# k^T v as the weight and q as the moving operand in the attention bursts of a fused attention and GLU kernel

## The chip, the cores and the metric

One Trainium2 chip, of which the kernel uses one core. The metric is device microseconds of one execution; before the change two runs took 1019.85 and 1017.05 us, median 1018.45. The profile is of one more execution, of 1019.05 us. Engines are named as in the profile: PE is TensorE, DVE VectorE, ACT ScalarE, POOL GpSimd; SP only issues DMAs.

## The reference

Linear attention without a softmax, an RMS norm over each head's 64 features, and a feed-forward layer whose gate is a sigmoid. All is fp32; the feed-forward weights come as 64-bit floats.

```python
def _attn_ref(q, k, v, g_norm):          # q, k, v: 8 batches, 8 heads, 576 tokens, 64 features
    kv = np.einsum('bhsd,bhse->bhde', k, v)
    out = np.einsum('bhsd,bhde->bhse', q, kv)
    rms = np.sqrt(np.mean(out * out, axis=-1, keepdims=True) + 1e-06)
    return (out / rms * g_norm).astype(np.float32)
...
def _moe_ref(x, w_gate, w_val, w_out):   # x: 4608 tokens x 512; 512 x 1536 twice; 1536 x 512
    gate = 1.0 / (1.0 + np.exp(-(x @ w_gate)))
    val = x @ w_val
    return (gate * val @ w_out).astype(np.float32)
```

x is the attention's output with the heads side by side: 4608 rows (8 batches of 576 tokens), 512 columns.

## The kernel before

The feed-forward runs in nine chunks of 512 tokens, c = 0 to 8. Chunk 0 is computed with plain matmuls while the 64-bit weights are turned to fp32. Chunks 1 to 8 use a fast form of matrix multiplication: each layer is split in blocks, and 26 products of sums of blocks take the place of 32. `first_layer_fast` (products at L932) runs 3 x 26 products, of two matmuls each with 256 moving columns; `second_layer_fast` (products at L1029) runs 26 products of three blocks. Sums of blocks of x, of the weights and of h are formed by DVE and GpSimd (L722, L741, L830, L1003), and the products are combined out of PSUM by DVE (L902) and ACT (L898, L891 for the sigmoid). Five PSUM banks go round among the products; three more are one tile, `at`, of the attention.

The attention of batches 0 and 1 is computed at the start, by `attention`. That of batches 2 to 7 is spread over the first and second layers of the chunks: `feed(b)` makes a list of steps, and chunk c carries those of batch c + 1 (so chunks 1 to 6 carry batches 2 to 7). Where a step goes is written out by hand: a pair (p, i) in `first` says that step i is issued after product p of the first layer, counted 0 to 77; the steps in `then` go after products of the second layer, and the lists X1, X2, X3 and `forms` place the sums of x and of weights in the same way. Every engine does its instructions in the order in which they were issued, so a step also holds its place in its engine's queue. A step after product p is issued behind that product's own combining work.

For each batch there are:

- `kv_mm` (L366, L372) and `kv_copies` (L377, ACT): k^T v of all eight heads into `at`, and from there to `kvq`, with k's features on partitions, 32 at a time;
- `turn` (L383): DVE transposes q in 32 x 32 blocks into `qTs`;
- `two_pairs(n0)`, twice, for two pairs of heads each: `u_mm` (L407) computes u = q (k^T v) with tokens on partitions, 72 matmuls with 32 rows of contraction, 64 columns of q as the weight and 64 columns of k^T v moving; `u_square` (L413, ACT), `u_sum` (L416, DVE, twice), `u_root` (L419, ACT), `u_norm` (a reciprocal at L423 and twice L425, DVE), and twice `x_turn`: DVE transposes of 32 x 32 blocks into `xTs` (L432), and DMAs on SP's queue (L442) that carry them to `xT_ring`, where the feed-forward reads x with features on partitions.

Since `at` is one tile, the second `u_mm` of a batch waits until the first pair's u has been read. The steps of the second `two_pairs` up to `u_norm` stand in the first layer, its two `x_turn` steps in the second layer. `load_q`, the stores of the output (L496, L503), and in chunk 1 the writes of the formed weights (L758, L1008) use SP's queue too; the streamed weights use GpSimd's (L770, L990).

Of the kernel before, what the change touches and what calls it, by code (L numbers as in the profile page):

```python
# [10 lines left out]
FP32 = mybir.dt.float32  # L11
# [3 lines left out]
AF = mybir.ActivationFunctionType  # L15
ALU = mybir.AluOpType
AX = mybir.AxisListType
# [3 lines left out]
def kernel(  # L21
# [11 lines left out]
    nc = tc.nc  # L33

    B, H, S, HD = q.shape
    T, DM = out.shape
    DF = moe_w_gate.shape[1]
    P = 128
    NHP = H // 2
    NJ = 6  # L40
    NP = S // NJ
    JH = NJ // 2


    PH = P // 2
# [5 lines left out]
    QB = 32  # L51
    NQ = NP // QB
    QC = QB * NJ
    NC = HD // QB
    XC = QB * JH
# [6 lines left out]
    G = 512  # L62
# [8 lines left out]
    const = ctx.enter_context(tc.tile_pool(name="const", bufs=1))  # L71
    sb = ctx.enter_context(tc.tile_pool(name="sb", bufs=2))
# [173 lines left out]

    qTs = const.tile([P, 2, 2 * NJ * HD], FP32, name="qTs")
    sqs = const.tile([P, 2 * NU * P], FP32, name="sqs")
    xTs = const.tile([P, NC, 2, S // 2], FP32, name="xTs")
    for e in range(2):  # L250
        nc.scalar.dma_start(out=g_col[HD * e:HD * e + HD], in_=g_norm.rearrange("(d o) -> d o", o=1))
    make_identity(nc, ident)
    nc.vector.memset(eps, 1e-6)

    nc.scalar.activation(out=sb.tile([P, 1], FP32, name="unused", bufs=1), in_=eps, func=AF.Sqrt)
# [2 lines left out]
    NX = 3  # L258
# [95 lines left out]
    def feed(b):  # L354
# [33 lines left out]
        def two_pairs(n0):  # L388


            d = {}
            ms = sb.tile([P, NQ, NJ], FP32, tag="ms2", name="ms2", bufs=1)
            sq = sqs[:, 0:2 * S].rearrange("p (r c) -> p r c", r=NQ)
            units = [slice(NJ // 2 * i, NJ // 2 * (i + 1)) for i in range(2)]

            def by_head(t):
                return t.rearrange("p r (n d) -> p r n d", d=HD)

            def u_mm():
                d["u"] = u = at_ps()[:, 0:NQ, 0:2 * QC]  # L400
                for which in range(2):
                    for g in range(JH):
                        for i in range(NC):
                            for r in range(NQ):
                                for e in range(2):
                                    c, o = NJ * HD * e + QC * i + PH * g, HD * (JH * which + g)
                                    nc.tensor.matmul(u[HD * e:HD * e + HD, r, o:o + HD],  # L407
                                                     qTs[QB * r:QB * r + QB, (n0 + which) % 2, c:c + PH],
                                                     kvq[QB * r:QB * r + QB, (n0 + which) % NHP, NC * e + i],
                                                     start=(i == 0), stop=(i == NC - 1))  # L410

            def u_square():
                nc.scalar.activation(out=sq, in_=d["u"], func=AF.Square)  # L413

            def u_sum(i):
                nc.vector.tensor_reduce(out=ms[:, :, units[i]], in_=by_head(sq)[:, :, units[i]], axis=AX.X, op=ALU.add)  # L416

            def u_root():
                nc.scalar.activation(out=ms, in_=ms, func=AF.Sqrt, bias=eps, scale=1.0 / HD)  # L419

            def u_norm(i):
                if i == 0:
                    nc.vector.reciprocal(ms, ms)  # L423
                m_ = ms[:, :, units[i]]
                nc.vector.tensor_tensor(out=by_head(sq)[:, :, units[i]], in0=by_head(d["u"])[:, :, units[i]],  # L425
                                        in1=m_.unsqueeze(3).to_broadcast([P, NQ, NJ // 2, HD]), op=ALU.mult)

            def x_turn(i):


                for which in range(2):
                    nc.vector.transpose(xTs[:, i, which],  # L432
                                        sq.rearrange("p r (w g i c) -> p w i r g c", w=2, g=JH, i=NC)[:, which, i])
                m = n0 % NHP
                for j in range(2):
                    for e in range(2):
                        p0, p1 = HD * e + QB * j, HD * e + QB * i
                        s0 = 0
                        while s0 < S // 2:
                            o = (S * b + S // 2 * j + s0) % (NX * G)  # L440
                            n_ = min(NX * G - o, S // 2 - s0)
                            nc.sync.dma_start(out=xT_ring[p1:p1 + QB, m:m + 2, o:o + n_],  # L442
                                                          in_=xTs[p0:p0 + QB, i, :, s0:s0 + n_])
                            s0 += n_

            return ([u_mm, u_square, lambda: u_sum(0), lambda: u_sum(1), u_root, lambda: u_norm(0), lambda: u_norm(1)] +
                    [lambda i=i: x_turn(i) for i in range(NC)])

        def turns_of(n):
            return [lambda n=n, e=e: turn(n, e) for e in range(2)]  # L450
# [3 lines left out]
        t0, t1, t2, t3 = (turns_of(n0 + i) for i in range(4))  # L454
        u0, u1 = two_pairs(n0), two_pairs(n0 + 2)
        steps_ = t0 + t1 + t2 + t3 + u0 + u1[:7]
        first = [(p, steps_[i]) for p, i in (((0, 0), (5, 1), (9, 2), (21, 3), (25, 8), (26, 9), (28, 4), (28, 5), (30, 10), (30, 11), (32, 6), (42, 12), (48, 13), (49, 7), (50, 14), (52, 15), (53, 16), (53, 17), (56, 18), (57, 19), (57, 20), (60, 21), (60, 22), (62, 23)) if b == 2 else
                                             ((4, 0), (8, 1), (24, 2), (24, 3), (28, 8), (29, 4), (29, 5), (30, 9), (32, 10), (33, 11), (35, 6), (37, 12), (41, 13), (47, 7), (47, 14), (51, 15), (51, 16), (53, 17), (56, 18), (56, 19), (56, 20), (60, 21), (60, 22), (65, 23)) if b == 3 else
                                             ((3, 0), (7, 1), (24, 2), (24, 3), (28, 8), (28, 4), (30, 5), (30, 9), (30, 10), (32, 11), (37, 12), (39, 6), (47, 13), (47, 7), (47, 14), (53, 15), (53, 16), (54, 17), (56, 18), (56, 19), (56, 20), (60, 21), (61, 22), (63, 23)))]
        return kv, first, u1[7:]  # L460

    def flush():
# [24 lines left out]
    def store(c, t, ot, cols=slice(0, DM), queues=(nc.sync,)):  # L487

        r0 = i = 0
        while r0 < P:  # L490
            b, s = divmod(G * c + P * t + r0, S)
            rows = out[S * b:S * b + S, cols]
            if b < 2:
                j, p = divmod(s, NP)
                n = min(P - r0, NP - p)
                queues[i % len(queues)].dma_start(out=rows.rearrange("(p j) d -> j p d", j=NJ)[j, p:p + n],  # L496
                                                  in_=ot[r0:r0 + n, cols])
            else:

                half, c0 = divmod(s, S // 2)  # L500
                r, c0 = divmod(c0, XC)
                n = QB
                queues[i % len(queues)].dma_start(  # L503
                    out=rows.rearrange("(r p g i) d -> i r g p d", p=QB, g=JH, i=2)[half, r, c0 // QB],
                    in_=ot[r0:r0 + n, cols])
            r0 += n
            i += 1

# [17 lines left out]
    def at_ps():  # L526
        return psum.tile([P, NQ, 512], FP32, tag="at", name="at")
# [567 lines left out]
        store(0, t, ot)  # L1095

    flush()
    X1 = (12, 16, 16, 17, 18, 18, 19, 19, 19, 20, 20, 21, 21, 24, 25, 25, 25, 25)
    X2 = (14, 15, 16, 17, 19, 21, 24, 25, 25, 25, 25, 25, 25, 25, 25, 25, 25, 25)
    X3 = (7, 8, 11, 11, 12, 13, 14, 14, 16, 16, 19, 22, 22, 22, 22, 22, 23, 23)  # L1100
    for c in range(1, NG):
        at1, at2 = {}, {}
        if c + 1 < B:
            kv, first_, then = second_batch if c == 1 else feed(c + 1)
            for p, step in (list(zip((19, 21, 21, 24, 26) if c == 2 else (19, 20, 22, 25, 25), kv)) if c > 1 else []) + first_:
                at1.setdefault(p, []).append(step)
            for p, step in zip((3, 6) if c == 1 else (4, 6), then):
                at2.setdefault(p, []).append(step)
        if c + 1 < NG:
            for n, p in enumerate(X1 if c == 1 else X2 if c + 1 < B else X3):  # L1110
                at2.setdefault(p, []).append(lambda n=n, c=c: x_sum(c + 1, n))
        if c == 1:
            for at_, forms in ((at1, ((28, 9, 0), (30, 10, 0), (34, 12, 0), (52, 8, 1), (56, 13, 0), (58, 14, 0), (64, 16, 1), (66, 11, 1), (74, 19, 0))), (at2, ((1, 22, 0), (3, 23, 1), (4, 25, 1), (7, 21, 1), (9, 15, 0), (10, 24, 0), (10, 20, 0), (11, 17, 0), (12, 18, 0)))):
                for p, n, pool_ in forms:
                    at_.setdefault(p, []).append(lambda n=n, eng=nc.gpsimd if pool_ else nc.vector: w_form(n, eng))
        first_layer_fast(c, at1)
        if c == 1:
            sgs += [spare_sg] + more_sgs
        second_layer_fast(c, at2)
# [30 lines left out]
```

## Time and profile before

| | |
|---|---|
| time, median of 2 runs | 1018.45 us |
| profiled execution | 1019.05 us |
| its span, first to last instruction | 1017.3 us |
| granted TensorE clock, mean over the span | 1.000 |
| idle of TensorE at the two longest waits after 261 us | 2.18 and 0.93 us |
| DMA traffic | 193.89 MB, mean 191 GB/s |
| L407, busy, records | 22.2 us, 1728 |
| L932 and L1029 on the chain that ended last | 46% and 24% of the span |

In the profile's groups a line gives the source line, engine, operation, the tile written and those read, the shape, the count; then the busy time in us, the mean ns of one, and the idle time before them with what ended it. A timeline line gives the start in us, the length up to the last end, and the same. A line of DMA issues gives the tile written and read, the issuing queue, the count, the KB of each, and the median us from issue to landing. A line of windows gives, for a stretch, its length, the busy time and count of each of PE, PE's weight load, DVE, ACT and POOL, then the granted clock, the share of time in which the DMA engines were busy, and GB/s. The matmuls of TensorE overlap, so its busy time in itself says little; the pitch from one start to the next is what a matmul costs.

### The profile page before, as it was taken

The numbers are of one execution on the slowest core, as the hardware profiler recorded it, in microseconds if no ns is written. First come the engines' busy times: TensorE is split into PE (matmuls) and PEld (weight loads), VectorE is DVE, ScalarE is ACT, GpSimd is POOL, SyncE is SP. The second block draws the span as 40 slices with busy tenths as digits, with TensorE's granted clock in tenths as the row PEclk, the third lists the DMA queues.
The fourth block names the chain that finished last, engine by engine and source line by source line (L and its number), as shares of the span: only waits on it lengthen the run. The fifth ranks groups of instructions, "written<-read, shape, count | busy, mean of one in ns | idle before, by whom it ended". The sixth has DMA issues, their size and how long they took to land.

```text
span 1017.3 us, 18352 instructions
## 1 busy us (share of the span) xinstructions
PE 1005.9 (99%) x6914; PEld 827.5 (81%) x6914; DVE 728.1 (72%) x1211; ACT 350.2 (34%) x609; POOL 602.4 (59%) x965
## 2 busy tenths in 40 slices
PE   8999999999999999999999999999999999999998
PEld 7644447888878888888888888888888888888887
DVE  4799899899758846775668666866688466755672
ACT  4654422442144304541254115421553033203320
POOL 0000999998539651867177706952496439743963
PEclk9999999999999999999999999999999999999999
DMA  9975315645876568646675577656765545454614
GB/s 267 272 234 192 124 42 160 217 133 183 273 256 224 164 198 262 232 159 197 210 252 178 164 224 231 211 157 184 239 203 162 186 159 202 162 157 159 208 59 126
DMA packets 101128, 193.89 MB, mean 191 GB/s; under 512 B 27408, under 2 KB 74128, under 8 KB 101040
## 3 DMA queue, kind: packets, MB, share of 16 engines
q0 software_dynamic: 20976, 112.87, 33.1%
q1 hardware_dynamic: 72896, 77.75, 25.1%
q10 hardware_dynamic: 7168, 2.10, 0.9%
q8 instruction: 55, 0.90, 0.4%
q14 instruction: 33, 0.27, 0.1%
HBM read 160.04 MB, written 25.56 MB: 182 GB/s over the span
## 4 chain that ended last, share of the span: by engine, by line
PE 73%; POOL 2%; DMA 1%; issue 0%; DVE 0%; POOLq 0%
PE mm L932 46%; PE mm L1029 24%; PE at L407 2%; POOL h L722 1%; DMA h_more<-in_v_dram 1%; PE at L366 1%; POOL w_ring L1003 0%; POOL h_more L722 0%; PE at L372 0%; POOL w L770 0%; DVE sg L902 0%; POOL w L1003 0%; POOLq L1003 0%
## 5 line engine op out<-in xcount | busy, mean ns | idle before, releaser
L932 PE MATMUL mm<-xs,w 128*128 128x256 f32 x1428 | 331.7, 380 | 0.0
L932 PEld LDWEIGHTS mm<-xs,w 128*128 128x128 f32 x1428 | 270.6, 190 | 37.0
L932 PE MATMUL mm<-xT,w 128*128 128x256 f32 x948 | 230.1, 380 | 0.0
L932 PEld LDWEIGHTS mm<-xT,w 128*128 128x128 f32 x948 | 179.3, 190 | 25.5 <-issue 1.0
L902 DVE TENSOR_TENSOR sg<-sg,mm 128x512 f32<-128x512 f32 (+1 forms) x176 | 100.8, 600 | 95.7 <-PE mm L932 49.9
L770 POOL DMA_DIRECT2D w<-kept x84 | 47.1, 561 | 190.2 <-PE mm L932 188.6
L1029 PE MATMUL mm<-w,h 128*128 128x256 f32 x630 | 143.4, 379 | 1.4 <-POOL h L722 0.9
L1029 PEld LDWEIGHTS mm<-w,h 128*128 128x128 f32 x630 | 119.5, 190 | 18.4 <-POOL h L722 1.3
L898 ACT COPY temps<-mm 128x512 f32<-128x512 f32 (+1 forms) x128 | 66.0, 538 | 189.7 <-PE mm L1029 94.7
L894 POOL TENSOR_TENSOR h<-h,sg 128x512 f32<-128x512 f32 x72 | 97.7, 1373 | 49.8 <-DVE h L902 34.1
L722 POOL TENSOR_TENSOR h<-h 128x128 f32<-128x128 f32 x216 | 115.7, 548 | 16.5 <-DVE h_more L722 13.1
L1029 PE MATMUL mm<-w,h_more 128*128 128x256 f32 x474 | 108.2, 379 | 0.0
L891 ACT ACTIVATE sg<-sg 128x512 f32<-128x512 f32 x96 | 59.7, 630 | 135.0 <-DVE sg L902 135.0
L1029 PEld LDWEIGHTS mm<-w,h_more 128*128 128x128 f32 x474 | 90.1, 190 | 12.2
L898 ACT COPY sg<-mm 128x512 f32<-128x512 f32 (+1 forms) x112 | 57.0, 510 | 90.9 <-PE mm L1029 48.7
L722 POOL TENSOR_TENSOR h_more<-h 128x128 f32<-128x128 f32 x120 | 58.7, 492 | 34.4 <-DVE h L894 30.0
L561 PE MATMUL mm<-xT,w 128*128 128x512 f32 x176 | 77.7, 594 | 0.0
L902 DVE TENSOR_TENSOR temps<-temps,mm 128x512 f32<-128x512 f32 (+1 forms) x96 | 59.3, 618 | 25.6 <-PE mm L1029 17.6
L902 DVE TENSOR_TENSOR temps<-mm,temps 128x512 f32<-128x512 f32 (+1 forms) x64 | 39.8, 622 | 51.2 <-PE mm L1029 23.6
L898 ACT COPY h<-mm 128x512 f32<-128x512 f32 x48 | 28.0, 586 | 128.0 <-PE mm L932 112.5
L741 POOL TENSOR_TENSOR h_more<-w 128x256 f32<-128x256 f32 x10 | 12.9, 1300 | 97.8 <-PE at L366 97.8
L902 DVE TENSOR_TENSOR sg<-mm,sg 128x512 f32<-128x512 f32 (+1 forms) x64 | 39.5, 618 | 39.8 <-PE mm L932 20.7
(132 smaller groups left out, 1325.4 us busy)
## 6 DMA issues: line engine op xcount, KB each, us to landing
w<-kept POOLq DMA_DIRECT2D x42, 896.0 KB, 5.3
w<-kept POOLq DMA_DIRECT2D x90, 384.0 KB, 4.7
w<-kept POOLq DMA_DIRECT2D x42, 768.0 KB, 5.4
q<-in_q_dram SPq DMA_DIRECT2D x24, 288.0 KB, 3.1
out_dram<-sg SPq DMA_DIRECT2D x104, 64.0 KB, 1.7
st<-in_moe_w_gate_dram SPq DMA_DIRECT2D x12, 512.0 KB, 5.0
st<-in_moe_w_val_dram SPq DMA_DIRECT2D x12, 512.0 KB, 6.7
h_more<-in_k_dram SPq DMA_DIRECT2D x24, 256.0 KB, 5.4
```

The lines of the kernel that those rows point to most:

```text
L366: nc.tensor.matmul(ps[HD * e:HD * e + HD, n // 2, n % 2], mains[n, "k"][:, c], mains[n, "v"][:, c], start=(n % 2 == 0 and j == 0), stop=Fa ...
L407: nc.tensor.matmul(u[HD * e:HD * e + HD, r, o:o + HD], qTs[QB * r:QB * r + QB, (n0 + which) % 2, c:c + PH], kvq[QB * r:QB * r + QB, (n0 + ...
L561: nc.tensor.matmul(self.ps[i], w[("wg", "wv")[i], self.f][:, m, :], xT[self.c][:, m, :], start=(m == 0), stop=(m == NMT - 1), skip_group_c ...
L722: ops.append((eng, lambda v=v, x=x, sign=sign, y=y, eng=eng: eng.tensor_tensor(out=h_form(v, j), in0=h_form(x, j), in1=h_form(y, j), op=op ...
L741: nc.gpsimd.tensor_tensor(out=w1_slot(j, w_at[v]), in0=w1_slot(j, w_at[x]), in1=w1_slot(j, w_at[y]), op=op_of(sign))
L770: nc.gpsimd.dma_start(out=granule(g)[:, 0:n], in_=kept1[g // NPA % N3, g % NPA][:, 0:n])
L891: nc.scalar.activation(out=o["o" + step[1]], in_=o["o" + step[1]], func=AF.Sigmoid)
L894: mult.tensor_tensor(out=o[x], in0=o[x], in1=o[y], op=ALU.mult)
L898: nc.scalar.copy(out=o[out_], in_=o[expr])
L902: tt(out=o[out_], in0=o[x], in1=o[y], op=ALU.add if sign == "+" else ALU.subtract)
L932: nc.tensor.matmul(regions[name][1][:, g], ws[:, g], xf[c][wv], start=(new and g == 0), stop=True, skip_group_check=True)
L1029: nc.tensor.matmul(regions[name][1], h_form(hv, j), ws[:, j], start=(used[i] and j == 0), stop=(j == N3 - 1), skip_group_check=True)
```

## The change

- `u_mm` swaps its operands: k^T v (64 columns) is the weight, q (192 columns) moves. u then has the features of two heads on partitions and tokens along the row; there are 24 matmuls instead of 72.
- The sum over features is now one over partitions. `u_sum` makes it by 12 matmuls with `head_ones` as weight (128 x 32, ones where a row belongs to a head), into the free end of the tile `at`. `head_ones` is set once, by memsets on GpSimd.
- `u_root` and `u_inverse` work on 128 x 96 values. `keep` writes the factors of the norm to a tile in device memory, four DMAs of 6 x 96 values; `spread` reads them back, two DMAs, each spreading its rows over 64 partitions.
- `x_out` multiplies u, out of PSUM, by the spread factors, and writes `xT_ring` itself; the transposes and the DMAs of `x_turn` are gone, and the tile `xTs` with them.
- The order of tokens in a batch's columns changes, and `store` with it.
- The lists of places are new for the three kinds of chunk, for k^T v, for the sums of x, and for the weights formed in chunk 1; two of the latter move from GpSimd to DVE on balance.

```diff
-            def u_mm():
-                d["u"] = u = at_ps()[:, 0:NQ, 0:2 * QC]
-                for which in range(2):
-                    for g in range(JH):
-                        for i in range(NC):
-                            for r in range(NQ):
-                                for e in range(2):
-                                    c, o = NJ * HD * e + QC * i + PH * g, HD * (JH * which + g)
-                                    nc.tensor.matmul(u[HD * e:HD * e + HD, r, o:o + HD],
-                                                     qTs[QB * r:QB * r + QB, (n0 + which) % 2, c:c + PH],
-                                                     kvq[QB * r:QB * r + QB, (n0 + which) % NHP, NC * e + i],
-                                                     start=(i == 0), stop=(i == NC - 1))
+            norms = kept_pool.tile([2 * NQ, 4, QC // 2], FP32, name=f"norms{n0}")
+            def u_mm():
+                d["at"] = at_ps()
+                d["u"] = d["at"][:, 0:NQ, 0:2 * QC]
+                for which in range(2):
+                    for i in range(NC):
+                        for r in range(NQ):
+                            for e in range(2):
+                                c = NJ * HD * e + QC * i
+                                nc.tensor.matmul(d["u"][HD * e:HD * e + HD, r, QC * which:QC * which + QC],
+                                                 kvq[QB * r:QB * r + QB, (n0 + which) % NHP, NC * e + i],
+                                                 qTs[QB * r:QB * r + QB, (n0 + which) % 2, c:c + QC],
+                                                 start=(i == 0), stop=(i == NC - 1))
...
+            def u_sum():
+                d["ms"] = d["at"][:, 0, 2 * QC:2 * QC + QC // 2]
+                for r in range(NQ):
+                    for i in range(4):
+                        nc.tensor.matmul(d["ms"][QB * i:QB * i + QB], head_ones[:, r],
+                                         sq[:, r, QC // 2 * i:QC // 2 * (i + 1)], start=(r == 0), stop=(r == NQ - 1),
+                                         skip_group_check=True)
...
+            def u_inverse():
+                nc.vector.reciprocal(rms, rms)
+            def keep():
+                for i in range(4):
+                    nc.sync.dma_start(out=norms[:, i], in_=rms[QB * i:QB * i + 2 * NQ])
+            def spread():
+                for e in range(2):
+                    nc.sync.dma_start(out=sq[HD * e:HD * e + HD],
+                                      in_=norms.rearrange("(r e) i c -> e r (i c)", e=2)[e].partition_broadcast(HD))
+            def x_out(which):
...
+                    nc.vector.tensor_tensor(
+                        out=xT_ring[:, m + which, o:o + QC * n_].rearrange("p (r c) -> p r c", c=QC),
+                        in0=d["u"][:, r0:r0 + n_, cs], in1=sq[:, r0:r0 + n_, cs], op=ALU.mult)
```

Places in the first layer of chunks 3 to 6, as product numbers; steps 0 to 7 are turns, 8 to 16 the first two pairs, 17 to 23 the second up to the last that stands there:

```diff
-((3, 0), (7, 1), (24, 2), (24, 3), (28, 8), (28, 4), (30, 5), (30, 9), (30, 10), (32, 11), (37, 12), (39, 6), (47, 13), (47, 7), (47, 14), (53, 15), (53, 16), (54, 17), (56, 18), (56, 19), (56, 20), (60, 21), (61, 22), (63, 23))
+((7, 0), (9, 1), (24, 2), (24, 3), (28, 8), (29, 4), (30, 5), (30, 9), (31, 10), (34, 11), (34, 12), (38, 13), (39, 6), (40, 14), (41, 7), (43, 15), (43, 16), (49, 17), (50, 18), (54, 19), (56, 20), (56, 21), (56, 22), (57, 23))
```

Before, steps 8 to 16 are u_mm, Square, two sums, Sqrt, two norms, two x_turns; after, u_mm, Square, u_sum, Sqrt, reciprocal, keep, spread, two x_outs. k^T v starts after product 20 instead of 19 in chunks 2 to 6, and its copies move with it. In chunk 2 the steps from u_mm to the second u_mm stand after products 28, 31, 32, 33, 34, 35, 37, 47, 48 and 52, the second Square and u_sum after 53 and 54; in chunk 1 they stand after 26, 29, 30, 33, 33, 34, 36, 41, 42 and 52.

## The prediction

> **What bounds the kernel now.** I read the page first: the busy row, then the chain of work that ended last, in order of time.
>
> ```profile
> PE 1005.9 (99%) x6914; PEld 827.5 (81%) x6914; DVE 728.1 (72%) x1211; ACT 350.2 (34%) x609; POOL 602.4 (59%) x965
> ...
> 811.33 67.34 PE mm L932 x312
> ```
>
> TensorE bounds it. From 261 us on the chain is TensorE almost alone. The second row gives the unit: 67.34 / 312 = 0.216 us per record of 256 moving columns (0.84 ns a column). An fp32 matmul leaves two records (L407: 1728 = 12 bursts x 72 matmuls x 2), so a product of the first layer, two matmuls, is 4 x 0.216 = 0.863 us. I count places in the first layer by products, 0 to 77. DVE at 72% is cover, not the bound: what is saved there is worth nothing unless TensorE waits for it.
>
> Next the timeline of TensorE around one attention burst of chunk 4 (start, length to the last end, records), and where it waits outright:
>
> ```profile
> 515.70 0.38 PE L932 MATMUL mm<-xT,w 128*128 128x256 f32 x1
> 516.01 1.85 PE L407 MATMUL at<-kvq,qTs 32*64 32x64 f32 x144
> 517.79 0.70 PE L932 MATMUL mm<-xs,w 128*128 128x256 f32 x2
> ...
> 505.63 2.08 PE L366 MATMUL at<-h_more 128*64 128x64 f32 x64
> 507.65 0.46 PE L372 MATMUL at<-h_more 64*64 64x64 f32 x16
> ...
> 218.55 1.13 PE L932 MATMUL mm<-xs,w_ring 128*128 128x256 f32 x4 [0.77 <-ACT sg L898]
> ...
> 261.24 1.99 PE L1029 MATMUL mm<-w,h 128*128 128x256 f32 x8 [0.93 <-POOL h L722]
> ...
> 292.00 0.69 PE L366 MATMUL at<-h_more 128*64 128x64 f32 x16 [2.18 <-DMA h_more<-in_v_dram]
> ```
>
> A burst costs more than its records. Before it, a start is 0.31 instead of 0.216 after the last one (0.09 lost). Its starts spread over 1.63 (1.85 less the 0.217 that one record lasts); its last start is 0.15 before the next product; and the first two L932 records after it start 0.70 - 0.38 = 0.32 apart (0.10 lost). Together 0.09 + 1.78 + 0.10 = 1.98 us, twelve times. The clock row shows 9 in all 40 slices, so no clock effect enters.
>
> **Part 1, u_mm: 72 matmuls of 64 columns become 24 of 192.** 64 columns alone would take 54 ns; here a start comes every 11.4 ns (1.63 / 143), so 4.7 of the six tiles (three row groups by two column halves) run together; 24 rounds of six take 68 ns each. A round of 192 columns is 162 ns at 0.84 ns a column, with 5 ns for the six starts 167; eight rounds are 1.34 us. With 0.09 and 0.10 at the ends, 0.09 to drain and 0.05 for a slow first round: 1.68 us, 0.30 less per burst. Ends: all six overlap and nothing else, 1.6; or again only 4.7 of six, 48 x 162 / 4.7 = 1.65, then 1.94. I take 1.68, since a long round leaves more time for the next weights.
>
> [...]
>
> **Part 2, u_sum: 12 new matmuls on TensorE** (K 128, 32 weight columns, 96 moving columns; 24 records), a mode change of their own, between products. One record alone is 81 ns. Nearest rows: L372, four tiles, 16 records whose starts spread over 0.24, one per 16 ns where 54 is the price alone: 3.3 together; L366, K 128 like u_sum but two column tiles, (2.08 - 0.22) / 63 = 29.6 ns: 1.8 of two. So column tiles do overlap. With four together six rounds of 86 ns are 0.52, and with the ends (0.09 + 0.10 + 0.09 + 0.05) 0.86 us. Ends: 0.75 (no slow first round, cheaper drain) and two at a time, 12 x 86 + 0.34 = 1.4. A gain is excluded: these are added records on an engine with no idle time there. I take 0.86, by L372's four tiles.
>
> Per burst 1.68 + 0.86 - 1.98 = +0.56; twelve times **+6.7 us** (ends 12 x 0.37 = +4.4 and 12 x 1.36 = +16).
>
> **Part 3, DVE's work, priced at nothing while TensorE covers it.** Groups, with mean ns:
>
> ```profile
> L432 DVE STREAM_TRANSPOSE xTs<-sqs 128x288 f32<-128x288 f32 x48 | 19.2, 445 | 0.0
> L425 DVE TENSOR_TENSOR sqs<-at,ms 128x576 f32<-128x576 f32 x24 | 17.9, 746 | 0.4
> L416 DVE TENSOR_REDUCE ms<-sqs 128x9 f32<-128x576 f32 x24 | 17.4, 747 | 11.8 <-ACT sqs L413 11.8
> L423 DVE RECIPROCAL ms<-ms 128x18 f32<-128x18 f32 x12 | 3.1, 258 | 0.0
> L323 DVE RECIPROCAL ms<-ms 128x10 f32<-128x10 f32 x8 | 1.7, 212 | 1.0 <-ACT ms L319 1.0
> ```
>
> Removed: 19.2 + 17.9 + 17.4 + 3.1 = 57.6 us. Added: x_out, 24 x 0.75 = 17.9 (a little more where the ring wraps), and 12 reciprocals of 96 elements, by the slope of the last two rows (46 ns for 8 elements) 0.71 each, 8.5. So about 31 us less DVE, worth 0. ACT keeps Square and Sqrt.
>
> **Part 4, the new waits.** (a) u_sum stands in TensorE's order behind Square, and the next product behind u_sum. In chunk 4 Square began 0.18 after the burst's last start and takes 1.13; u_sum comes three products (2.59) after the burst, so about 1.3 to spare; in the tightest place (chunk 2, second burst) two products, 1.73, some 0.4 to spare. Cost 0; if ACT were a copy (0.59) late, 0.2 there, once. (b) The second u_mm writes the PSUM tile that x_out reads, and x_out waits for two trips through device memory. Durations:
>
> ```profile
> q<-in_q_dram SPq DMA_DIRECT2D x24, 288.0 KB, 3.1
> out_dram<-sg SPq DMA_DIRECT2D x104, 64.0 KB, 1.7
> ...
> h_more<-in_k_dram SPq DMA_DIRECT2D x24, 256.0 KB, 5.4
> ...
> 524.00:528.00 4.00, 4.00 (x20) 3.54 (x19) 2.94 (x5) 2.77 (x4) 3.90 (x8) 1.00 0.91 312
> ```
>
> In chunk 4: product 28 ends at 516.0, product 29 starts at 517.5, u_sum ends about 521.0, Sqrt (table load 1.28, then 0.4) at 523, product 34's DVE sum ends at 524.4, reciprocal 525.1. keep: four issues of about 0.32 on SP, landing 1.7 later, 528.1. spread: issued by 528.8 and landed after 3.1 (q's row) to 5.4 (k's row, in the busy DMA of the last row above, share 0.91): 531.9 to 534.2. DVE reaches x_out after product 43, at 531.3, so it stands idle up to 2.9 us there, with its sums of products 44 on behind it; x_out ends at 533.4 to 535.7. u_mm is due after product 49, at 536.5: 0.8 to 3.1 to spare. As for the sums behind: product 48's ran at 537.42 in the old trace, 2.3 us after that product ended and no product waited, and DVE has 3 us less to do there. On SP, which stops at each wait, one q load stands behind keep and spread, due in the next chunk; in chunk 1 the writes of the formed weights too, some 4 us later than now and due in chunk 2. Cost 0; I take +1 over all chunks, as chunk 1 has two waits of half a microsecond to a microsecond already (0.77 above) and x_out as early as product 41. Ends 0 and, at the longest landing of the removed xT copies (7.4), 4 x 1.2 = +5.
>
> [...]
>
> **Part 5, moved steps.** k^T v of chunk 2 goes from after product 19 to after 20: its wait of 2.18 for v shrinks by up to 0.86: -0.9 (ends -2.2 and +1). In chunk 1 GpSimd forms two weight sums fewer (1.8 us each), ahead of its 0.93 wait; others move: 0 (ends -2 and +3). The memsets at the start lie on an idle GpSimd: 0. The stores change their rows, not their number.
>
> **Sum**, against the profiled execution (span 1017.3, time 1019.05): 6.7 + 1.0 - 0.9 = +6.8, 1025.9. The median of the runs is 0.6 lower: **1025.3 us**.
>
> **Rivals.** *The wait for spread becomes the bound* (the other side). Place: second u_mm after product 49 in chunks 3 to 6. Price 4 x (landing - 6.2). It makes the kernel slower by over 2% (about what a measurement of this kernel tells from no change; above 1038.8) from 3.4 us lost in each, a landing of 9.6 us. For it: DMA share 0.91 just then, and a q load once took 10.1. Against: medians of 3.1 and 5.4. At 10.1 it gives 1041. Chance 0.09. *u_sum's column tiles run one at a time*: 24 x 86 + 0.34 = 2.4 us, 12 x 2.1 = +25, 1044; decides from 2.0 us per u_sum. Against: L366 and L372. 0.05. *Overlap as poor as the bounds* (1.94 and 1.4): 1035. 0.13. *The cost goes with the number of records, not columns*: 72 instead of 144 at 11.4 ns, 0.82 + 0.60 with ends, -0.56 x 12: 1012. For it: starts 7 to 11 ns apart; against: 64 columns already take 54 ns alone, so a tile cannot take 192 sooner. 0.08. Forecast: 0.65, with 1019 to 1031 of its own.
>
> Range 1014 to 1039. Over 2% faster (below 998) needs more than all bursts cost (12 x 1.98 = 24 less the new ones): 0.02. Slower: half of the first rival's cases and more, all of the second and tails, 0.13. Within: 0.85.
>
> **What would show it.** In the profile after: bursts of 48 records about 1.5 us from first start to the next product, of 24 records about 0.67; no wait of TensorE on ACT's Square or on DVE's x_out; DVE busy near 697; a short idle of DVE before x_out on the DMA of sqs. I am wrong if the 24 records take 1.2 or more, or if TensorE waits before a second u_mm.

## The result and the profile after

The changed kernel took 1056.09 us, median of two runs (1051.71 and 1060.47), against 1018.45 before: a ratio of 1.0368, 95% interval 1.026 to 1.0475. It is slower, and outside the range of the prediction. The profiled execution is the one of 1051.71 us, 32.7 more than the profiled one before (1019.05); its span is 1049.9 us, its mean granted clock 0.988 (before 1.000).

First the page of the changed kernel: the busy row and the clock row.

```profile
PE 1024.4 (98%) x6050; PEld 834.8 (80%) x6050; DVE 702.4 (67%) x1149; ACT 349.9 (33%) x609; POOL 600.0 (57%) x970
...
PEclk9999999999999999899998999899999999999999
```

DVE lost 26 us, nearly as forecast, and it bought nothing. TensorE is busy 18.5 us more with 864 records fewer. The clock row, 9 throughout before, has three 8s. They stand within chunks 3 to 5.

The change's own bursts, in the timeline of TensorE in chunk 4 (start, length to the last end, records), and the new groups of DVE:

```profile
525.96 1.54 PE L409 MATMUL at<-qTs,kvq 32*64 32x192 f32 x48
527.43 2.86 PE L934 MATMUL mm<-xs,w 128*128 128x256 f32 x12
530.22 0.70 PE L421 MATMUL at<-sqs,head_ones 128*32 128x96 f32 x24
530.85 1.35 PE L934 MATMUL mm<-xs,w 128*128 128x256 f32 x5
```

```profile
L446 DVE TENSOR_TENSOR xT<-at,sqs 128x576 f32<-128x576 f32 x16 | 11.4, 746 | 17.2 <-DMA sqs<-norms 17.2
L429 DVE RECIPROCAL sqs<-sqs 128x96 f32<-128x96 f32 x12 | 9.0, 750 | 15.8 <-ACT sqs L426 15.7
```

u_mm takes 527.43 - 525.96 = 1.47 to the next product, u_sum 0.63. So the matmuls cost what was forecast. But x_out waits for `sqs`, the spread factors: 17.2 us of idle DVE stand ahead of its whole-width form alone, and in chunk 4 6.23 ahead of another form:

```profile
549.36 1.55 DVE L446 TENSOR_TENSOR xT<-at,sqs 128x192 f32<-128x192 f32 x4 [6.23 <-DMA sqs<-norms]
```

The chain that ended last shows the same chunk from the first u_sum on (start, us, what; the dots stand for pieces of up to 0.69 us):

```profile
530.92 2.80 PE mm L934 x12
...
534.53 0.68 DVE sqs L429
...
536.22 5.94 DMA norms<-sqs
...
542.87 6.40 DMA sqs<-norms
...
549.63 1.29 DVE xT L446 x3
...
550.97 2.85 PE at L409 x48
553.82 6.14 PE mm L934 x20
```

Before, this stretch of the chain was TensorE alone. Now it leaves TensorE at 533.7, goes through reciprocal, keep (L433), a trip of 5.94 us to device memory, spread (L437), a trip of 6.40 us back and x_out, and comes to TensorE again at 550.97. The second u_mm stands behind x_out, and the products stand behind that u_mm in TensorE's order. The waits of the whole program (total, times, longest):

```profile
DVE xT L446 <- DMA sqs<-norms: 23.4, 5, 6.2
...
PE at L409 <- DVE xT L446: 14.7, 4, 4.3
```

Four waits, one in each of chunks 3 to 6. They are not the whole loss. The last two rows of the chain are slow too: a second burst of 2.85 instead of 1.47, and 20 records in 6.14, 0.307 each instead of 0.216. The windows of TensorE over this stretch show why (from:to, length, busy and count, granted clock, DMA share, GB/s):

```profile
550.00:550.50 0.50, 0.00 (x0) 0.75 0.82 330
...
551.00:553.00 2.00, 2.00 (x42) 0.50 0.03 11
553.00:556.50 3.50, 3.50 (x25) 0.50 0.00 0
...
557.00:557.50 0.50, 0.50 (x4) 0.92 0.00 0
```

By the shares of the first and last of these windows the clock stood at half speed from 550.25 to 557.08, 6.8 us. TensorE worked through 6.1 of them (from 550.97): some 3 us lost behind a wait of 4.3.

**Where the 32.7 us went.** Chunk lengths, from the first product of one first layer to that of the next:

| chunk | 1 | 2 | 3 | 4 | 5 | 6 | 7 |
|---|---|---|---|---|---|---|---|
| before | 108.18 | 109.92 | 107.51 | 107.52 | 107.86 | 107.51 | 101.01 |
| after | 109.59 | 109.27 | 114.61 | 115.92 | 115.55 | 114.12 | 101.01 |
| after, second pairs later (below) | 109.54 | 109.39 | 108.61 | 108.61 | 108.61 | 108.61 | 101.01 |

The third row is an experiment in which no burst of chunks 3 to 6 waits: 108.61, so 1.10 per chunk for its two pairs of bursts. Against it chunks 3 to 6 lose 6.00 + 7.31 + 6.94 + 5.51 = 25.76 us. Of that TensorE's gaps at the four places, measured from start to start less what one record takes, are 3.27 + 4.47 + 3.69 + 3.96 = 15.4; the other 10.4 fit the half clock behind them, at which TensorE worked 5.9 + 6.1 + 6.8 + 3.4 = 22.2 us, 11.1 more than at the full clock. With 4 x 1.10 for the bursts, +1.41 in chunk 1, -0.65 in chunk 2 and +2.1 ahead of chunk 1 the sum is 33.0; the profiled executions differ by 32.7, and the 0.3 between is chunk 5 of the kernel before, 107.86 where its neighbours have 107.5. Chunk 7 carries no attention and did not change.

### The profile page after: what moved, and what is told of

Same layout as the page of the kernel before. It is cut to its first block, busy times and chain, and to the rows that moved or that the text cites. A ratio compares the mean times of both kernels' runs of the same rounds, so it can differ in the third digit from the quotient of the medians.

```text
span 1049.9 us, 16514 instructions
## 1 busy us (share of the span) xinstructions
PE 1024.4 (98%) x6050; PEld 834.8 (80%) x6050; DVE 702.4 (67%) x1149; ACT 349.9 (33%) x609; POOL 600.0 (57%) x970
## 4 chain that ended last, share of the span: by engine, by line
PE 89%; DMA 6%; DVE 2%; SPq 1%; issue 1%; ACT 0%; ACTq 0%; DVEq 0%
PE mm L934 46%; PE mm L1031 26%; PE mm L563 7%; PE mm L810 4%; DMA norms<-sqs 2%; DMA sqs<-norms 2%; PE at L409 2%; PE at L370 1%; DMA q<-in_q_dram 1%; PE at L421 1%; PE at L563 1%; DVE xT L446 1%; DVE h L904 0%; PE two L310 0%; DVE sg L904 0%
## 5 line engine op out<-in xcount | busy, mean ns | idle before, releaser
L934 PE MATMUL mm<-xs,w 128*128 128x256 f32 x1428 | 338.6, 384 | 2.2 <-DVE temps L904 2.2
L934 PEld LDWEIGHTS mm<-xT,w 128*128 128x128 f32 x948 | 182.4, 192 | 26.1 <-issue 0.5
L904 DVE TENSOR_TENSOR sg<-sg,mm 128x512 f32<-128x512 f32 (+1 forms) x176 | 100.8, 599 | 107.8 <-PE mm L934 48.7
L724 POOL TENSOR_TENSOR h_more<-h 128x128 f32<-128x128 f32 x120 | 64.4, 539 | 36.6 <-DVE h L896 28.4
L904 DVE TENSOR_TENSOR temps<-temps,mm 128x512 f32<-128x512 f32 (+1 forms) x96 | 59.5, 620 | 29.6 <-PE mm L934 13.8
L904 DVE TENSOR_TENSOR temps<-mm,temps 128x512 f32<-128x512 f32 (+1 forms) x64 | 39.9, 624 | 51.1 <-PE mm L1031 23.6
L904 DVE TENSOR_TENSOR sg<-mm,sg 128x512 f32<-128x512 f32 (+1 forms) x64 | 39.4, 616 | 51.8 <-PE mm L934 29.6
```

Of the source, the lines that this page charges most:

```text
L724: ops.append((eng, lambda v=v, x=x, sign=sign, y=y, eng=eng: eng.tensor_tensor(out=h_form(v, j), in0=h_form(x, j), in1=h_form(y, j), op=op ...
L904: tt(out=o[out_], in0=o[x], in1=o[y], op=ALU.add if sign == "+" else ALU.subtract)
L934: nc.tensor.matmul(regions[name][1][:, g], ws[:, g], xf[c][wv], start=(new and g == 0), stop=True, skip_group_check=True)
```

## The experiments

Theory: keep and spread land late because the streamed weights fill the DMA engines just then; the second u_mm waits for them, and half clock comes behind the wait. Rivals: keep stands behind other work on SP; the short rows of keep are slow in themselves; the new bursts are what costs. The ratios, against the kernel before, are those on record; they are not always the quotient of the two medians given.

**1. No streamed weights from chunk 3 on.** Edit of the changed kernel:

```diff
-        if g < N_GRAN:
+        if g < NPA * N3:
...
-        if i < N_FAST * NS:
+        if i < NS:
```

The feed-forward of the later chunks then computes with the weights that are left in their tiles, so that their output is not the reference's.

> The changed kernel, but GpSimd loads no streamed weights from chunk 3 on; chunks 3 to 8 then compute with the weights that chunk 2 left, so their output is not the reference's. Theory (keep and spread queue behind the weight stream in the DMA engines): from keep's first issue to spread's first issue 2.3 to 2.6 us in chunks 3 to 6 as in chunk 1, instead of 6.6 to 7.5; no wait of TensorE before the second u_mm; 1051.7 less 4 x 6.6 = about 1025 us. Rival (the two trips are slow by their own form, 6 rows of 384 B, or by SP's queue): the trips stay at 6 to 7 us and the time within 3 us of 1052.

Measured: 1028.53 us, one run. The issues of keep and spread on SP in chunk 4, first of the changed kernel, then of this one:

```profile
535.23 1.29 SPq L433 DMA_DIRECT2D norms<-sqs  x4
542.24 1.41 SPq L437 DMA_DIRECT2D sqs<-norms  x2
```

```profile
531.58 1.29 SPq L433 DMA_DIRECT2D norms<-sqs  x4
533.83 1.24 SPq L437 DMA_DIRECT2D sqs<-norms  x2
```

Spread starts when keep has landed. That is 7.0 us after the first issue with the stream and 2.25 without. From spread's first issue to x_out it is 7.1 with the stream. Without it, it is 5.5 (533.83 to 539.37), and that only bounds the landing, since x_out starts right behind a sum of DVE and waits for nothing:

```profile
539.37 1.54 DVE L446 TENSOR_TENSOR xT<-at,sqs 128x192 f32<-128x192 f32 x4
```

TensorE waits for x_out nowhere in chunks 3 to 6. So the stream makes 4.8 of keep's 7.0 us and at least 1.6 of spread's 7.1. The rest of spread's time, at most 5.5, is not the stream's; it loads 288 KB twice. The program itself has the same contrast: in chunk 1, which streams no weights, keep takes 2.44 and 2.33 in the changed kernel. The time is 3.5 us above the expected 1025: chunk 2 is 112.89 long instead of 109.27, by a wait of 1.92 and half clock behind it (last section). The DMA part of the page for 535 to 543 us (packets, MB, share of 16 engines) shows what lies between:

```profile
q0 software_dynamic: 436, 2.28, 82.6%
...
q1 hardware_dynamic: 48, 0.01, 0.6%
```

Queue q0 carries the weights: 2.28 MB / 436 = 5.2 KB a packet, and 0.826 x 16 x 8 us / 436 = 0.24 us each. The 48 of q1 are keep's: 0.006 x 16 x 8 / 48 = 0.016 us each. So the rows of 384 B are not slow here; they stand behind others. Keep's packets ran between 538.0 and 541.9, though the first was issued at 535.23. In experiment 1 the same 48 ran between 532.0 and 533.5, with the first issue at 531.58.

Keep's first packet ran 2.8 us after its first issue (538.0 against 535.23), in experiment 1 0.4 after (532.0 against 531.58). In what order a DMA engine takes the packets of several queues no run here showed.

**2. The second pairs later.** Chunks 3 to 6 only; steps 15 to 23 move, and nothing else:

```diff
-(43, 15), (43, 16), (49, 17), (50, 18), (54, 19), (56, 20), (56, 21), (56, 22), (57, 23)
+(54, 15), (54, 16), (58, 17), (59, 18), (63, 19), (65, 20), (65, 21), (65, 22), (66, 23)
```

> Only places change: in chunks 3 to 6 x_out stands after product 54, the second u_mm after 58 and what follows up to spread after 59 to 66 (instead of 43, 49, 50 to 57). Theory (the loss is the wait for the two trips and the low clock behind it): keep and spread still take 6 to 7 us each, the waits of 3.2 to 4.4 us and the slow bursts are gone, about 1025 us (1022 to 1029). Rival (the new bursts or DVE's work cost more than was seen, wherever they stand): above 1045.

Measured: 1026.37 us (1025.37 to 1027.13), ratio 1.0078, interval 1.0061 to 1.0095. TensorE in chunk 4:

```profile
544.15 3.62 PE L934 MATMUL mm<-xs,w 128*128 128x256 f32 x16
547.70 1.54 PE L409 MATMUL at<-qTs,kvq 32*64 32x192 f32 x48
```

The burst follows its product at full clock. The trips themselves are as long as ever (keep 6.7 to 7.5 us in these chunks); they are only covered. So 30 of the 38 us of loss lie in where the second pair stands, and the 8 us left are what the change costs with the waits for x_out covered (6.8 in the profiled spans, 1024.1 against 1017.3). The bursts make 6 x 1.10 = 6.6 of them.

**3. Filler matmuls ahead of the second u_mm** in chunks 3 to 6, 14 of 128 x 128 x 128 into a free end of the tile `at`, so that TensorE would work through the wait:

```diff
+            def filler(n):
+                for _ in range(n):
+                    nc.tensor.matmul(d["at"][:, 1, 2 * QC:2 * QC + P], ident, ident, start=True, stop=True,
+                                     skip_group_check=True)
...
+            def filled_u():
+                u0[9](14)
+                second_u()
```

> In chunks 3 to 6, 14 matmuls of 128 x 128 x 128 on the identity (3.0 us at the full clock) are added ahead of the second u_mm, into columns of the PSUM tile that nobody reads. Theory (after a wait of some 4 us the clock is granted at about half for some 6 us, which costs about 2.5 us a chunk beside the wait): TensorE stands idle for about 1.3 us only, the clock stays at 1.00, the burst is 1.22 us from first to last start instead of 2.3, and the time falls by 4 x 2.5 to about 1042, though there is more work. Rival (burst and products after it are slow for another reason, such as PSUM shared with DVE): 1052 or more, up to 1064 if the filler is not hidden.

Measured: 1061.17 us (1057.77 to 1064.85), ratio 1.042, interval 1.0387 to 1.0453. The expectation missed, since the filler writes the same tile that x_out reads, and so waited as the u_mm had:

```profile
550.83 6.14 PE L453 MATMUL at<-ident 128*128 128x128 f32 x28 [3.60 <-DVE xT L446]
557.02 1.55 PE L409 MATMUL at<-qTs,kvq 32*64 32x192 f32 x48
...
787.02 3.39 PE L453 MATMUL at<-ident 128*128 128x128 f32 x28 [2.02 <-DVE xT L446]
```

It does tell one thing apart. Now the filler is the slow work behind the wait (28 records from 550.83 to 557.02, 0.22 each where 128 columns at 0.84 ns are 0.11), and the u_mm of 1.55 right behind it runs at full speed. In chunk 6, the last row, the clock stayed at 1.00 behind a wait of 2.02, and the same filler took 0.12 a record. So the slowness is the half clock after a wait, not the form of u_mm or of the filler.

**4. Keep issued from ACT's queue**, for the rival that it stands behind other work on SP:

```diff
-                    nc.sync.dma_start(out=norms[:, i], in_=rms[QB * i:QB * i + 2 * NQ])
+                    nc.scalar.dma_start(out=norms[:, i], in_=rms[QB * i:QB * i + 2 * NQ])
```

> keep's four DMAs are issued from ACT's queue instead of SP's, all else as in the changed kernel. Theory (the packets wait in the DMA engines, which all queues share): keep's way stays at 5 to 7.5 us in chunks 3 to 6, the time between 1048 and 1060. Rival (SP's queue holds them): keep takes about 2.4, TensorE's waits fall to under 1 us, about 1030.

Measured: 1053.19 us, one run. Keep and spread in chunk 4, then the waits of TensorE:

```profile
536.66 2.00 ACTq L433 DMA_DIRECT2D norms<-sqs  x4
...
542.85 1.24 SPq L437 DMA_DIRECT2D sqs<-norms  x2
```

```profile
PE at L409 <- DVE xT L446: 13.2, 4, 4.7
PE mm L934 <- ACT sg L900: 6.6, 4, 1.7
```

Keep takes 4.6, 6.2, 5.3 and 4.9 us in chunks 3 to 6, where it took 7.5, 7.0, 6.6 and 7.3 from SP. That is shorter, two of the four under the 5 that the theory gave as the least, but about twice the 2.4 of the rival; the wait stays, and ACT, which spends 2.00 us on the four issues (SP 1.29), makes products wait besides, 6.6 us in four. So SP's order is not the main cause. Whether it held part of the 1.8 us between the two means, or keep met another moment of the stream, was not tried.

**5. The second layer's weights loaded later** in chunks 3 to 6, behind the trips of the first pair instead of over them (from product 46 on, not 20); all is computed:

```diff
-                    k_, r = divmod(p - 20, 2)
+                    k_, r = divmod(p - (46 if 2 < c < B - 1 else 20), 2)
```

> In chunks 3 to 6 GpSimd issues the seven loads of 384 KB for the second layer after products 46 to 58 instead of 20 to 32; the loads for the first layer stay. Theory (keep and spread queue behind the weight stream): with part of the stream gone from their time, keep takes 2.5 to 5 us instead of 6.6 to 7.5, x_out ends earlier, the waits before the second u_mm shrink from 3.2 to 4.4 us to between 0 and 2, time 1027 to 1037. Rival (only the place of the burst matters, the way through device memory is as long without that traffic): 1050 or more.

Measured: 1029.81 us, one run. Chunk 4:

```profile
528.00 1.29 SPq L433 DMA_DIRECT2D norms<-sqs  x4
531.15 1.23 SPq L437 DMA_DIRECT2D sqs<-norms  x2
```

Keep lands after 3.15 (2.7 to 3.4 in chunks 3 to 6, at a DMA share of 0.53 to 0.61 instead of 0.83 to 0.88). From spread's first issue to x_out it is still 7.2 to 8.3; in chunk 4 the weights' queue then took 36.7% of the DMA engines' time (531.0 to 538.3). The waits for x_out fall to 3.2 us in four, the longest 1.71, and the clock stayed at 1.00 through them. So keep's landing is set by what is queued, also in a kernel that leaves nothing out.

**6. Part 5 by itself.** The kernel before, k^T v of chunk 2 later: first at three products later, then at the places of the changed kernel, then with the first u_mm later too.

```diff
-(19, 21, 21, 24, 26) if c == 2
+(22, 24, 24, 25, 26) if c == 2
```

> The kernel before, in which k^T v of chunk 2 stands after product 22 instead of 19 and its copies after 24, 24, 25 and 26. Theory (the 2.18 us that TensorE waits there for v are a wait for a fixed landing, not a queue that moves along): the wait is gone, 1016.3 us, a ratio of 0.998. Rival: the wait turns up at ACT's copies, which the first u_mm of the chunk needs: within 0.5 of the kernel before.

Measured: 1017.92 against 1018.51 us, ratio 0.9989, interval 0.9977 to 1.0002. The rival held. Waits, and the clock behind them:

```profile
PE at L407 <- ACT kvq L377: 1.5, 1, 1.5
...
PE at L366 <- DMA h_more<-in_v_dram: 0.4, 1, 0.4
```

```profile
300.00:302.00 2.00, 2.00 (x139) 0.85 0.03 8
302.00:304.00 2.00, 2.00 (x6) 0.50 0.78 203
304.00:306.00 2.00, 2.00 (x8) 0.80 1.05 351
```

The wait for v went from 2.18 to 0.4, and one of 1.5 came for ACT's copies of k^T v, with some 3.4 us of half clock behind it. In the kernel before, the clock stood at 1.00 after its 2.18. This profile is of an execution of 1019.71 us with a mean clock of 0.998; seven of the twelve had 1.000, so the half clock is not in all of them.

```diff
-(19, 21, 21, 24, 26) if c == 2
+(20, 22, 24, 26, 27) if c == 2
```

> The kernel before, with one edit: k^T v of chunk 2 takes the places that the changed kernel gives it (products 20, 22, 24, 26, 27 in place of 19, 21, 21, 24, 26). Theory (Part 5's term is real by itself): the wait of 2.18 us for v goes to 0 to 0.4, and a wait of 0.5 to 1.0 us for ACT's copies comes ahead of u_mm, as in the changed kernel (0.69); net 0.8 to 1.6 us less, ratio 0.9984 to 0.9992. Rival (as with the places 22, 24, 24, 25, 26: the copies give back what the wait for v gains): ratio 0.9995 or more, a wait for the copies of 1.5 us or more.

Measured: 1018.82 against 1019.82 us, ratio 0.9995, interval 0.9979 to 1.0012. No difference is shown:

```profile
PE at L366 <- DMA h_more<-in_v_dram: 2.3, 2, 1.3
...
PE at L407 <- ACT kvq L377: 0.5, 1, 0.5
```

The wait for the copies is in the range of the theory. The one for v is not: it is still 1.26 in chunk 2, where the theory had at most 0.4. In this execution (1022.33 us) chunk 2 begins 2.1 us later than in the profile before, and the wait for v ends 2.05 later (294.05 against 292.00). So v's landing is not fixed; it moved with the program.

```diff
-(19, 21, 21, 24, 26) if c == 2
+(21, 23, 23, 25, 26) if c == 2
...
-(28, 8), (29, 4), (29, 5), (30, 9), (32, 10)
+(30, 8), (31, 4), (31, 5), (32, 9), (33, 10)
```

> The kernel before, with k^T v of chunk 2 after products 21, 23, 23, 25, 26 and its first u_mm two products later (after 30 instead of 28; the turns of the third pair, Square and the first sum one or two later with it). Theory: both waits go, the one for v (2.18 us) and the one for ACT's copies, so 1.8 to 2.2 us less: ratio 0.998. Rival: a new wait of 1 us or more comes behind it in the same chunk, at the second u_mm or at a product whose bank DVE or ACT frees late; ratio 0.999 to 1.001.

Measured: 1019.40 against 1019.82 us, ratio 1.0002, interval 0.999 to 1.0013: the rival, though its new wait, at a product ahead of the moved burst, is a little under the 1 us it named:

```profile
PE mm L932 <- ACT h L898: 0.9, 1, 0.9
```

None of the three beats the kernel before.

**7. The second pair three products later**, in chunks 3 to 6, for the least move that might do:

```diff
-(43, 15), (43, 16), (49, 17), (50, 18), (54, 19), (56, 20), (56, 21), (56, 22), (57, 23)
+(46, 15), (46, 16), (52, 17), (53, 18), (57, 19), (59, 20), (59, 21), (59, 22), (60, 23)
```

> As the changed kernel, but in chunks 3 to 6 x_out stands after product 46, the second u_mm after 52 and what follows three products later too. x_out still ends about 4.4 us after product 49 is due, so 1.8 us after product 52. Theory (even a wait of 2 us is followed by a granted clock of about 0.5 for some us, as in chunk 2 of the kernel without the stream): about 1.8 of wait and 1.5 to 2 behind it, four times, on top of 1026: 1038 to 1042. Rival (the clock falls only after waits of over 3 us): 1026 + 4 x 1.8 = 1033 or less.

Measured: 1050.27 us (1047.28 to 1051.07), ratio 1.03, interval 1.0275 to 1.0325. The expectation missed. TensorE, then DVE, in chunk 4:

```profile
541.49 1.03 PE L934 MATMUL mm<-xs,w 128*128 128x256 f32 x4
547.72 2.07 PE L934 MATMUL mm<-xs,w 128*128 128x256 f32 x4 [5.20 <-DVE sg L904]
549.59 3.14 PE L934 MATMUL mm<-xT,w 128*128 128x256 f32 x8
552.66 1.54 PE L409 MATMUL at<-qTs,kvq 32*64 32x192 f32 x48
```

```profile
545.52 1.55 DVE L446 TENSOR_TENSOR xT<-at,sqs 128x192 f32<-128x192 f32 x4 [4.91 <-DMA sqs<-norms]
546.99 1.47 DVE L904 TENSOR_TENSOR sg<-sg,mm 128x512 f32<-128x512 f32 x2
```

The u_mm waits no longer; a product does, the third ahead of it. By the program, product 50 adds into a PSUM bank that DVE first has to read for a sum after product 47, and that sum stands in DVE's order behind x_out, which waits. So x_out's place binds the products themselves, wherever u_mm stands. Moving x_out past the landing (experiment 2) frees both.

## Why the prediction was wrong

**The step that failed is Part 4(b), the landings.** It had keep land 1.7 us after its issues and spread 3.1 to 5.4 after its own, x_out done at 533.4 to 535.7 and u_mm due at 536.5, so "Cost 0; I take +1 over all chunks". Counted from keep's first issue, that allowed 6.8 to 9.1 us to x_out, with 9.9 before TensorE waits. The profile shows 14.1 (535.23 to 549.36), 4.2 too many: the wait of 4.3. Keep was the larger error: 7.0 from first issue to landing where the prediction's terms make 1.3 + 1.7 = 3.0, while spread's 7.1 to x_out was 1.0 beyond the 0.7 + 5.4 of the far end (and at most 5.5 without the stream). With keep's error alone even the near end, 6.8, becomes 10.8, and TensorE waits.

The cause lies in the row chosen for keep. The 1.7 is the median of the stores of the output, and those stand in the second layer. In the trace before, chunk 4's were issued from 587.7 to 598.8, where the DMA share was 0.54 (588 to 598), and at 524 to 528, where keep would stand, it was 0.91. A small size does not bring the 1.7 about either, as the rows of the removed xT copies had shown: of 48 and 24 KB, smaller than a store's 64, they landed after 3.1 and 3.2.

```profile
588.00:598.00 10.00, 10.00 (x48) 8.79 (x47) 4.77 (x14) 0.59 (x1) 0.00 (x0) 1.00 0.54 163
...
xT<-xTs SPq DMA_DIRECT2D x16, 24.0 KB, 3.2
```

The range of that step named the 7.4 of the longest such copy, but charged it once, for spread, though both trips run while the weights' queue fills the DMA engines (82.6% of their time from 535 to 543 us).

**A second term was missing: the clock behind a wait.** "The clock row shows 9 in all 40 slices, so no clock effect enters" was true of the profiled execution, and the change made waits long enough to bring the half clock in. It turned 15.4 us of gaps into a loss of 25.8. Even the kernel before is not free of it: of its 17 executions beside experiments 5 to 7, eight had a mean clock of 1.000 and took 1018.1 us on the mean, seven had 0.996 to 0.998 and took 1020.9.

**The first rival is what happened**, in mechanism and place. Its price, 4 x (landing - 6.2), had keep's 1.7 in it as well, and left the clock out; so it named 1041 where the profiled execution took 1051.7. Its 4 x 3.9 = 15.6 us lie beside the 15.4 of gaps by luck: it gave spread a landing of 10.1, while most of the excess was keep's. Its chance of 0.09 leaned on medians.

**Parts 1 and 2 held.** Predicted was +0.56 for each u_mm with its u_sum; the chunk lengths give 1.10 / 2 = 0.55, 6.6 us for twelve against 6.7. By rows u_mm is 0.09 + 1.47 + 0.10 = 1.66 (1.68 predicted) and u_sum 0.09 + 0.63 + 0.10 = 0.82 (0.86), together 0.50 above the old 1.98. Six row and column tiles overlap, and four do: 48 records of 162 ns by their columns (7.8 us) took 1.47, and 24 of 81 ns (1.9 us) took 0.63 (u_sum's starts lie within 0.46 us, 20 ns each). The prediction's 5 ns for six starts and 0.05 for a slow first round were its estimates; no run shows either by itself. "The cost goes with the number of records", "u_sum's tiles run one at a time" and "overlap as poor as the bounds" fall by the same rows.

**Part 3 held**: 702.4 us of DVE (697 predicted; the reciprocal took 750 ns instead of 710, and one sum 3.3 us longer, see the end), and the 26 us less bought nothing. **Part 4(a) held**: no wait of TensorE on Square at a u_sum. **Part 5**, -0.9 for chunk 2: the chunk became 0.65 shorter with 1.1 of bursts in it, and it is 109.26 to 109.39 long in six of the seven profiles of the changed kernel and its variants; the runs of experiment 6 show no gain from such a move by itself, so which of the moves brought it stays open. Chunk 1 the sum had at 0 besides its bursts, and it came 0.3 longer than these (1.41 less 1.10). In experiments 5 and 7, with the same program up to chunk 2 and without the slow sum that the last paragraph tells of, it is 107.8 instead of 109.59. So that sum goes with 1.8 us, and the rest of the chunk gained 1.5. The 2.1 us more ahead of chunk 1 are within what executions differ by: chunk 1 starts between 162.2 and 164.8 in the four profiles of the kernel before and its variants, and between 163.2 and 164.8 in the seven of the changed kernel and its variants.

**The short rows of keep**, 384 B each, are no large cost here: without the weight stream keep lands in 2.25 us, issues included.

## What to carry to other kernels

Price a small transfer on a chain of waits by what else moves at its place in the schedule, not by another transfer's median elsewhere in the program: here keep took 7.0 us behind the weights and 2.25 without them, where the prediction's terms, borrowed from elsewhere, made 3.0. Where two trips stand in a row, give both the loaded price. Look for every engine that stands behind the consumer: in experiment 7 the wait left one instruction and came back at another, as DVE's order had not changed. And charge a wait of TensorE of a few us at more than its length, for the half clock that can follow: here 15.4 us of gaps became a loss of 25.8.

## What the runs showed of the hardware

**Half clock lasted 3.4 or 6.8 us here, behind waits as short as 1.5.** In the changed kernel it lasted 6.83 us in chunks 3, 4 and 5 and 3.41 in chunk 6, behind gaps of 3.27, 4.47, 3.69 and 3.96. In experiment 1 a single wait of 1.92 us in chunk 2 was followed by half clock too, which began 0.7 us after work had resumed:

```profile
326.50:327.00 0.50, 0.34 (x12) 1.00 0.04 12
...
327.25:327.50 0.25, 0.25 (x18) 0.85 0.78 129
...
328.00:330.00 2.00, 2.00 (x21) 0.50 0.11 38
...
330.50:331.00 0.50, 0.50 (x3) 0.66 0.00 0
```

The columns are those of the windows above: work resumes at 326.66 at full clock, which is half from about 327.4 to 330.8. The 1.51 of experiment 6 did the same, while 2.18 in the kernel before, 1.71 in experiment 5, 2.02 in experiment 3 and 2.32 and 2.44 in experiment 4 cost no clock. A wait of 2.1 to 2.2 us in chunk 1 was followed by half clock in experiment 4 (12 records in 4.54 us) and not in experiments 1 and 2 (12 in 2.86) and the changed kernel. So in these runs the length of a wait does not decide alone.

In the changed kernel the clock changes at 434.19, 441.02, 550.25, 557.08, 666.30, 673.13, 782.36 and 785.77. Its four stretches of half clock begin 116.06, 116.05 and 116.06 us apart, while the bursts behind the waits begin at 435.16, 550.97, 666.12 and 781.93, 115.81, 115.15 and 115.81 apart. So half clock does not begin at a fixed distance from the work behind the wait: it began 0.97 and 0.72 us before that work in chunks 3 and 4, and 0.18 and 0.43 after it had begun in chunks 5 and 6. What sets its moment and its length was not shown.

**One sum of DVE took 3.97 us instead of 0.7** (h<-h,temps at L904, at 200.99 in chunk 1 of the changed kernel; 3.9 in experiments 1 and 2, 2.75 in 4, and 0.9 in 3, 5 and 7), and TensorE waited 2.2 us behind it. In the changed kernel GpSimd adds beside it without a pause, in instructions of 0.47 and 0.74 us, up to 204.41; its first pause, of 0.08 us, begins there, and the sum ends 0.55 later. No run tried whether the two hang together, and the cause stays open.
